# One batch's tile sums computed as matrix products, and the next batch's pooling softmax and memories moved into the kernel's head

## The chip, the core and the metric

The kernel runs on one core of a Trainium2 chip. The core has a matrix engine (PE; the profile shows its weight loads apart as PEld), a vector engine (DVE), a scalar engine (ACT), GpSimd (POOL) and a sync engine (SP) that here issues every transfer. Each engine runs its own list of instructions in order and waits on semaphores for the others. The metric is the device time of one execution in microseconds.

## The reference

Eight batches of memory attention feed a Fourier mixing layer and a feed-forward layer. Cut to what matters:

```
a      = softmax(phi, over the 32 memories)            # phi: 8 x 8 x 576 x 32
k_m    = einsum('bhsm,bhsd->bhmd', a, k)               # 32 memories per head
v_m    = einsum('bhsm,bhsd->bhmd', a, v)
attn   = softmax(q @ k_m^T / 8)                        # 576 x 32 per head
x      = attn @ v_m, the eight heads side by side      # 8 x 576 x 512
u      = x + real(fft(fft(x, axis=seq), axis=model))
un     = (u - mean(u)) / sqrt(var(u) + 1e-6)
out    = u + relu(un @ w_ch1) @ w_ch2                  # 512 -> 2048 -> 512
```

The code subtracts the maximum of phi over the 576 positions (the softmax over axis 2 normalises over positions), and the sums are normalised with 1e-9 added.

## The kernel before

**Layout.** Heads are taken in pairs, so a batch has four pairs (`NG`), 128 partitions each. A batch first makes the pooling weights: phi is transposed on PE (tiles `pf`, `pl`), DVE takes maxima, ACT exponentiates into `pht`, and PE transposes back (`pt_e`) into `et`. Then each pair's memories are products of k and v with `et` (`pm`), its scores are products of q with the memories (`psc`), and `pair_scores` softmaxes them. The Fourier transform over positions is a product with a cosine and a sine table (`ct`); with cosines even and sines odd, the six tiles of a pair's attention weights `a` are first added and subtracted into even and odd parts `eo` (L524 to L531), split into f16 high and low parts `aeo` (L534 to L538), and multiplied in `spectrum` (`pa`, evicted into `at` at L618 and L619). `values` prepares the pooled values (`vh`), and `mix_m` and `mix_x` (`pp_t`, `px_t`) make the rows `u` in `uring`.

**Precision.** Batches 0 and 1 (`NX = 2`) work in float32; later ones split float32 into two f16 parts and make three f16 products.

**Feed-forward.** The rows are taken in 18 chunks of 256 (`CH = 2` tiles). Chunk 0 is computed in float32 directly (`ffn1_direct` L744, `ffn2_direct` L761) while the weights are being turned from 64-bit words into floats: `to_f32` (L842 to L855) for the eight units of W1 and of W2, one ACT and three DVE instructions per unit or half unit. Afterwards `split_w1` and `prepare_w2` split them into f16 high and low parts, and chunks 1 to 17 run three f16 products for each (L274 `ph` and L797 `po`).

**Order.** A framework's scheduler sets the order on each engine from the order in which the code issues, from priorities and from explicit edges (`issue_after`). The generator `background()` issues a batch's work in steps; the loop over chunk 0's eight units issues two steps of the second batch after each unit, and the chunks after it go on so. `GATE1` and `GATE2` name marks behind which a unit's conversion is issued: W2's unit 0 behind `at0`, the last spectrum eviction of the first batch.

**Fillers.** `keep_busy(n)` (L246) issues products of a zero tile of 512 columns into a PSUM tile that nobody reads. `KEEP` gives the counts: 8 before the first data, 18, 4 and 3 in the first batch's pooling, 14 in `values` of batch 0, and 19 ahead of chunk 0's normalised input `pt_unT` (L726).

**Second batch before the change.** `pooling_weights(1)` is issued behind `at0`, so its transposes, exponentials and copies run at the start of chunk 0, and its four pairs' memories run inside chunk 0, with masking by DVE (L396, L398). Its phi and its k, v, q come by transfers behind those of weight units 1 and 2 (L283, L295).

Of the kernel before, what the change touches and what calls it, by code (L numbers as in the profile page):

```python
# [10 lines left out]
F32 = mybir.dt.float32  # L11
F16 = mybir.dt.float16
# [121 lines left out]
def kernel(  # L134
# [43 lines left out]
    uring = const.tile([P, NU, DM], F32, name="uring")  # L178
    zeros = uring[:, NU - 1].bitcast(F16)[:, :DM]
    nc.vector.memset(zeros, 0.0)  # L180
    identf = const.tile([P, P], F32, name="identf")
    make_identity(nc, identf)
    make_identity(nc, ident)
    warm = const.tile([P, 1], F32, name="warm")
    nc.vector.memset(warm, 0.0)
# [192 lines left out]
    def memory_f32(b, g, r, vmf, parts):  # L378
# [15 lines left out]
        if 0 in parts:  # L394
            kmf = share[:, g * 64 : g * 64 + 64] if b == 0 else tiny("kmf", 64, 2)
            nc.vector.tensor_tensor(out=kmf, in0=pm[:, 0:64], in1=mk[:, 0:64], op=ALU.mult)  # L396
        if 1 in parts:
# [6 lines left out]
        return kmf  # L404

    def pair_memory(b, g, r, vmf, ivs):

# [67 lines left out]
    def pair_scores(b, g, q, sc, km, es, aeo):  # L475
# [37 lines left out]
        nc.vector.reciprocal(out=sm, in_=sm)  # L513
        eng = nc.gpsimd if b else nc.vector
        eng.tensor_tensor(out=a, in0=a, in1=sm.unsqueeze(2).to_broadcast([P, 12, M]), op=ALU.mult)  # L515

        av = a.rearrange("p (t h) m -> p t (h m)", h=2)
        ahl = ahring[:, (b * NG + g) % NAH]
        if b == 0 and g > 0:
            ahl = ud.rearrange("p l t c -> p (l t c)")[:, (g - 1) * 5 * P : g * 5 * P]  # L520
            ahl = ahl.rearrange("p (t c) -> p t c", t=5)
        nc.scalar.copy(out=ahl[:, :, 0:64], in_=av[:, 0:5])
        nc.gpsimd.tensor_tensor(out=ahl[:, :, 64:128], in0=av[:, 0:5], in1=ahl[:, :, 0:64], op=ALU.subtract)
        for i, op in ((12, ALU.add), (16, ALU.subtract)):  # L524
            eng.tensor_tensor(out=a2[:, i : i + 4], in0=a[:, 0:4], in1=a[:, 4:8], op=op)  # L525
        ap = a2[:, 8:].rearrange("p (t s h) m -> p t s (h m)", s=2, h=2)
# [3 lines left out]
        )  # L530
        nc.vector.tensor_tensor(out=eo[:, :, 1], in0=ap[:, :, 0], in1=ap[:, :, 1], op=ALU.subtract)  # L531
        hi, lo = (aeo[:, l].rearrange("p t e h c -> p (t e h) c")[:, :, g * M : g * M + M] for l in range(2))
        eov = eo.rearrange("p t e (h m) -> p (t e h) m", m=M)
        marks[f"a{b}_{g}"] = nc.scalar.copy(out=hi, in_=eov)  # L534
        nc.gpsimd.tensor_tensor(out=lo[:, 4:], in0=eov[:, 4:], in1=hi[:, 4:], op=ALU.subtract)
# [201 lines left out]
    def ffn1_direct(j):  # L737
# [3 lines left out]
        for f in range(UB):  # L741
            ph = ps1.tile([P, CH, P], F32, tag="h", name=f"ph_0_{j}_{f}", padded_shape=[P, 4, P])
            for k in range(NK):
                nc.tensor.matmul(  # L744
                    ph, lhsT=w[:, k, f * P : (f + 1) * P], rhs=unTs[0][:, k], start=(k == 0), stop=(k == NK - 1)
                )
            nc.scalar.activation(h[:, f], ph, AF.Relu)

# [181 lines left out]
    def background():  # L930
# [3 lines left out]
        for b in range(B):  # L934
# [6 lines left out]
            if b == 0:  # L941
# [63 lines left out]
    def load_unit(n, parts, w, stages):  # L1005
        marks["load"] = marks.get("load", marks["q"])
        parts[n] = load_stage(w[n], stage_area(stages[n]))

    def load_weights(n):

        for parts, w, stages in ((parts_w1, w1, W1_STAGE), (parts_w2, w2, W2_STAGE)):
            if n not in parts:
                load_unit(n, parts, w, stages)


    for what in [1, 'w1', 2, 3, 'w2']:
        if what == "w1":
            load_unit(0, parts_w1, w1, W1_STAGE)
            marks["q"] = marks["load"]
        elif what == "w2":  # L1020
            load_unit(0, parts_w2, w2, W2_STAGE)
            marks["q"] = marks["load"]
        else:
            first.append(load_pair(0, what))
            marks["load"] = marks["q"]
    marks["load"] = marks["q"]
    with tc.issue_after(marks["load"].ins):
        vts = [load_vt()]
        marks["load"] = nc.sync.dma_start(out=ct, in_=ct_d)
    for j in range(3):  # L1030
        load_weights(j)

# [137 lines left out]
```

## Time and profile before

| | us |
|---|---|
| median of 3 runs | 951.38 (951.35 to 952.24) |
| the profiled execution | 951.47 |
| its span, first to last instruction | 949.6 |
| transposes of chunk 0's input start | 50.50 |
| chunk 0's first product `ph` starts | 53.41 |
| chunk 0's last product `po` ends | 126.2 |
| the last `po` ends | 945.8 |

The span is what the trace covers; 1.9 us of the execution lie around it. In the profile's groups a row names line, engine, operation, tiles, shapes and count, then busy time, mean duration in ns, and idle time ahead of the group with its releaser. Rows of the timeline begin with start and duration in us; their count merges neighbours, and a float32 product counts twice, as it shows two records. In rows of windows the stretch stands first, then its length, then busy times with counts, the granted clock of PE as a share, the busy share of the DMA engines, and GB/s. DVE's durations overlap by about 0.1 us: the next instruction starts that much before the one ahead ends.

### The profile page before, as it was taken

How to read it: one execution, taken by the hardware profiler on the slowest of the kernel's cores; microseconds unless marked ns; L12 is line 12 of the kernel's file. 1: busy time of each engine (PE TensorE's matmuls, PEld its weight loads, DVE VectorE, ACT ScalarE, POOL GpSimd, SP SyncE). 2: the span in 40 equal slices, each digit the busy share in tenths (PEclk: the TensorE clock that was granted, in tenths of full speed). 3: DMA queues.
4: the chain of work that ended last, by engine and by line, in shares of the span. 5: the costliest groups of instructions: out<-in, count | busy, mean ns of one | idle time of the engine just before them, and what ended most of it. 6: DMA issues, size and time to landing. Idle time of an engine off the chain costs nothing.

```text
span 949.6 us, 18892 instructions
## 1 busy us (share of the span) xinstructions
PE 932.5 (98%) x7764; PEld 660.0 (70%) x7764; DVE 558.5 (59%) x1307; ACT 457.5 (48%) x912; POOL 216.3 (23%) x245
## 2 busy tenths in 40 slices
PE   9899999999999999999999999999999999999998
PEld 6566777577777777776767677777776667666664
DVE  5999878677565665667524676667656765221111
ACT  3565667865365545654514554755446544311110
POOL 1200442534122232323100241223221331200000
PEclk9999999999999999999999999999999999999999
DMA  9848551454126231643102631273223311110000
GB/s 343 308 170 266 178 145 19 86 134 103 43 45 172 55 93 26 156 113 93 23 23 54 143 96 48 48 155 95 45 68 72 82 20 36 39 45 23 1 23 23
DMA packets 115958, 88.08 MB, mean 93 GB/s; under 512 B 100384, under 2 KB 100384, under 8 KB 113824
## 3 DMA queue, kind: packets, MB, share of 16 engines
q1 hardware_dynamic: 115872, 86.87, 34.4%
q8 instruction: 61, 1.00, 0.4%
q14 instruction: 25, 0.20, 0.1%
HBM read 58.15 MB, written 9.44 MB: 71 GB/s over the span
## 4 chain that ended last, share of the span: by engine, by line
PE 88%; DVE 6%; DMA 2%; ACT 1%; POOL 1%; issue 1%; SPq 0%; DVEq 0%; POOLq 0%; ACTq 0%
PE po L797 36%; PE ph L274 35%; PE ph L744 3%; PE pm L274 3%; PE po L761 3%; PE pp_t L274 2%; PE psc L274 2%; PE px_t L274 2%; DMA w1t<-in_w 1%; PE pa L607 1%; PE pp_t L650 1%; PE pf L348 1%; PE pv L580 1%; POOL w2s L916 0%; DMA unring<-ud 0%
## 5 line engine op out<-in xcount | busy, mean ns | idle before, releaser
L274 PE MATMUL ph<-unring,w1t 128*128 128x256 f16 x3264 | 388.9, 273 | 2.9 <-DVE scratch L241 1.3
L797 PE MATMUL po<-w2s,hring 128*128 128x512 f16 x1632 | 378.5, 379 | 1.6 <-POOL w2s L916 1.6
L274 PEld LDWEIGHTS <-w1t 128*128 128x128 f16 x3264 | 314.9, 98 | 66.4 <-issue 4.8
L797 PEld LDWEIGHTS <-hring 128*128 128x128 f16 x1632 | 156.9, 98 | 160.0 <-issue 2.4
L788 DVE SCALAR_TENSOR_TENSOR hring<-ph,hring 128x512 f16<-128x512 f32 x136 | 93.1, 685 | 148.3 <-ACT hring L787 148.1
L787 ACT ACTIVATE hring<-ph 128x512 f16<-128x512 f32 x136 | 80.3, 591 | 166.4 <-PE ph L274 163.5
L710 POOL TENSOR_TENSOR scratch<-scratch,small 128x1 f32<-128x1 f32 x36 | 24.1, 670 | 197.6 <-DVE scratch L709 118.4
L515 POOL TENSOR_TENSOR aring<-aring,scratch 128x384 f32<-128x384 f32 x28 | 23.3, 833 | 183.5 <-DVE scratch L513 172.2
L274 PEld LDWEIGHTS <-stg 128*128 128x128 f16 x1152 | 44.7, 98 | 8.1
L509 ACT ACTIVATE aring<-aring,scratch 128x384 f32<-128x384 f32 x24 | 14.7, 612 | 63.1 <-DVE aring L508 63.1
L731 POOL TENSOR_TENSOR ud<-un,ud 128x1024 f16<-128x1024 f32 x17 | 36.7, 2158 | 30.6 <-ACT ud L730 30.6
L432 POOL TENSOR_TENSOR stg<-rawt,stg 128x640 f16<-128x640 f32 x12 | 18.3, 1524 | 86.9 <-ACT rawt L431 86.9
L274 PE MATMUL pm<-et,stg 128*128 128x64 f16 (+1 forms) x780 | 36.8, 199 | 0.0
L499 DVE TENSOR_REDUCE scratch<-psc 128x12 f32<-128x384 f32 x32 | 17.7, 554 | 32.4 <-PE pm L274 18.0
L534 ACT CAST aeo<-eo 128x384 f16<-128x384 f32 x30 | 15.3, 511 | 42.2 <-DVE eo L531 42.2
L686 DVE SCALAR_TENSOR_TENSOR uring<-px_t,scratch,share 128x256 f32<-128x256 f32 (+1 forms) x80 | 34.3, 478 | 0.1
L809 DVE SCALAR_TENSOR_TENSOR uring<-po,small,uring 128x512 f32<-128x512 f32 x34 | 24.2, 743 | 16.7 <-PE po L797 16.7
L672 DVE SCALAR_TENSOR_TENSOR share<-pp_t,scratch,small 128x257 f32<-128x257 f32 (+1 forms) x48 | 21.1, 483 | 20.9 <-ACT small L669 20.9
L525 POOL TENSOR_TENSOR aring<-aring 128x128 f32<-128x128 f32 x56 | 32.6, 602 | 2.1
L744 PE MATMUL ph<-unring,w1t 128*128 128x256 f32 x128 | 31.4, 389 | 0.0
L527 DVE TENSOR_TENSOR eo<-aring 128x128 f32<-128x128 f32 x29 | 28.1, 968 | 5.2 <-POOL aring L525 5.2
L536 DVE SCALAR_TENSOR_TENSOR aeo<-aeo,small,eo 128x128 f16<-128x128 f16 x30 | 24.3, 809 | 11.3 <-ACT aeo L534 11.2
(242 smaller groups left out, 1219.3 us busy)
## 6 DMA issues: line engine op xcount, KB each, us to landing
rawt<-in_raw SPq DMA_DIRECT2D x15, 640.0 KB, 5.2
stg<-in_raw SPq DMA_DIRECT2D x15, 640.0 KB, 4.8
out<-uring SPq DMA_DIRECT2D x36, 256.0 KB, 2.1
stg<-in_w SPq DMA_DIRECT2D x7, 1024.0 KB, 5.0
rawt<-in_raw SPq DMA_DIRECT2D x15, 384.0 KB, 3.5
stg<-in_raw SPq DMA_DIRECT2D x15, 384.0 KB, 3.1
phs<-in_raw SPq DMA_DIRECT2D x32, 160.0 KB, 4.1
w2s<-in_w SPq DMA_DIRECT2D x4, 1024.0 KB, 9.8
```

Of the source, the lines that this page charges most:

```text
L274: m = nc.tensor.matmul(out, lhsT=lhsT, rhs=rhs, start=start, stop=stop)
L525: eng.tensor_tensor(out=a2[:, i : i + 4], in0=a[:, 0:4], in1=a[:, 4:8], op=op)
L527: nc.vector.tensor_tensor(out=eo[:, 1:3, 0], in0=ap[:, 1:3, 0], in1=ap[:, 1:3, 1], op=ALU.add)
L536: marks[f"s{b}_{g}"] = nc.vector.scalar_tensor_tensor(out=lo[:, :4], in0=hi[:, :4], scalar=mk[:, 64:65], in1=eov[:, :4], op0=ALU.mult, op1 ...
L686: nc.vector.scalar_tensor_tensor(out=u[rows, hs], in0=px[rows, hs], scalar=igx[rows], in1=tm[rows, w * NJ + half : w * NJ + half + 256], o ...
L731: marks[f"ul{c}"] = nc.gpsimd.tensor_tensor(out=ud[:, 1], in0=un, in1=ud[:, 0], op=ALU.subtract)
L744: nc.tensor.matmul(ph, lhsT=w[:, k, f * P : (f + 1) * P], rhs=unTs[0][:, k], start=(k == 0), stop=(k == NK - 1))
L761: nc.tensor.matmul(po[t], lhsT=h[:, f, t], rhs=w[:, f], start=(j == 0 and f == 0), stop=(j == NW - 1 and f == UB - 1),)
L787: nc.scalar.activation(h[:, 0], phv, AF.Relu)
L788: nc.vector.scalar_tensor_tensor(out=h[:, 1], in0=phv, scalar=0.0, in1=h[:, 0], op0=ALU.max, op1=ALU.subtract)
L797: nc.tensor.matmul(po[t], lhsT=hs[j][:, lh, f * 2 + t], rhs=w2s[:, j * UB + f, lw, :], start=(j == 0 and f == 0 and i == 0), stop=(j == NW ...
L809: nc.vector.scalar_tensor_tensor(out=u, in0=po[t], scalar=cout if c else 0.5, in1=u, op0=ALU.mult, op1=ALU.add)
```

## The change

Three things change, and with them how the head is filled.

1. **Tile sums as products, batch 0.** DVE's and POOL's additions on `a` are not made for batch 0. Instead `a` is split into f16 high and low parts for all six tiles, and `tile_sums` adds up the even and odd parts in PSUM: products with the identity and with `minus`, its negative, one each for the high and the low part. The splits that follow read PSUM. POOL's remainders there go to DVE, and batch 0's masking of memories goes from DVE to ACT (two instructions of 64 partitions each, into tiles cleared before).
2. **Second batch in the head.** Its phi and its k and v are loaded right after the first batch's data (into areas that are free until chunk 0), its softmax over phi (`next_weights`) is issued after the tile sums, and its memories (`next_memories`) after chunk 0's normalisation; POOL masks them when a pair needs them. The scaling of the exponentials and the copies of the transposed ones go from DVE to ACT. Only q is loaded for it later.
3. **W2's first unit** is gated behind `s0_1`, the last part of pair 1's sums, in place of `at0`.

Fillers now multiply halves of the float identity, 256 columns each and twice as many; the 14 and the 19 go. Relu of chunk 0 gets a high priority.

```
-KEEP = [8, 18, 14, 0, 19, 4, 3]
+KEEP = [8, 18, 0, 0, 0, 4, 3]
-GATE2 = [["at0"]] + [["un1", "uh0"]] * 7
+GATE2 = [["s0_1"]] + [["un1", "uh0"]] * 7
...
-        pt = ps2.tile([P, 512], F32, tag="o", name=f"keep_{len(kept)}")
-        kept.append(pt)
-            for _ in range(n):
-                nc.tensor.matmul(pt, lhsT=zeros[:, :P], rhs=zeros, start=True, stop=True)
+            for _ in range(2 * n):
+                nc.tensor.matmul(idle, lhsT=unread[:, :P], rhs=unread, start=True, stop=True)
...
+        nt = 5 if b else 6
...
-        nc.scalar.copy(out=ahl[:, :, 0:64], in_=av[:, 0:5])
-        nc.gpsimd.tensor_tensor(out=ahl[:, :, 64:128], in0=av[:, 0:5], in1=ahl[:, :, 0:64], op=ALU.subtract)
+        nc.scalar.copy(out=ahl[:, :, 0:64], in_=av[:, 0:nt])
+        (nc.gpsimd if b else nc.vector).tensor_tensor(
+            out=ahl[:, :, 64:128], in0=av[:, 0:nt], in1=ahl[:, :, 0:64], op=ALU.subtract
+        )
+        if b == 0:
+            return ahl
...
+    def tile_sums(g, ahl, aeo):
+        pe = ps1.tile([P, 512], F32, tag="h", name=f"pe_{g}")
+        eo = pe[:, : 3 * P].rearrange("p (n c) -> p n c", c=2 * M)
+        for group in (
+            (
+                (ident, 0, slice(2, 6), 0, P),
+                (ident, 1, slice(2, 6, 2), 0, P),
+                (ident, 2, slice(2, 4), 0, P),
+                (ident, 3, slice(2, 6, 3), 0, P),
+                (minus, 1, slice(3, 6, 2), 0, P),
+                (minus, 2, slice(4, 6), 0, P),
+                (minus, 3, slice(3, 5), 0, P),
+            ),
+            (
+                (ident, 4, slice(0, 2), 0, 96),
+                (ident, 4, slice(1, 2), 96, P),
+                (ident, 5, slice(0, 1), 0, P),
+                (minus, 5, slice(1, 2), 0, P),
+            ),
+        ):
+            for i, (w, t, o, a, z) in enumerate(group):
+                for l in range(2):
+                    src = ahl[a:z, t, l * 64 : l * 64 + 64]
+                    marks["pe"] = nc.tensor.matmul(
+                        eo[:, o], lhsT=w[a:z],
+                        rhs=src.unsqueeze(1).to_broadcast([z - a, eo[:, o].shape[1], 64]),
+                        start=(i + l == 0), stop=(i + l == len(group)), skip_group_check=True,
+                    )
+        even_odd(0, g, eo.rearrange("p n (h m) -> p (n h) m", m=M), aeo, nc.vector)
...
+    def next_weights():
...
+            nc.scalar.activation(pht_next[:, g, : 4 * P], pf[g], AF.Exp, bias=m, accum_out=su[:, g : g + 1])
...
+            nc.scalar.activation(pht_next[:, g], pht_next[:, g], AF.Copy, scale=su[:, 2 + g : 3 + g])
...
+            nc.scalar.copy(out=et_next[g][:, :4], in_=pt.rearrange("p (t c) -> p t c", c=P))
...
+    def next_memories():
+        for g in range(NG):
+            kv = kv_next[g].rearrange("p (t w c) -> p t w c", t=NST, w=2)
+            pm = ps1.tile([P, 512], F32, tag="h", name=f"pm_1_{g}")
...
+            nc.scalar.copy(out=pm_next[:, g], in_=pm[:, :P])
...
-            return q, None, memory_f32(b, g, r, vmf, range(2)), 1.0 / 8.0
+            return q, None, kept_memory(g, vmf), 1.0 / 8.0
...
-            nc.scalar.activation(h[:, f], ph, AF.Relu)
+            with tc.high_priority(3000):
+                nc.scalar.activation(h[:, f], ph, AF.Relu)
...
                 for g in range(NG):
                     memory_f32(b, g, first[g], vmf, [1])
+                for g in range(NG):
+                    tile_sums(g, ahl[g], aeo)
+                next_weights()
...
-    for what in [1, 'w1', 2, 3, 'w2']:
+    for what in (1, 'w1', 2, 3, 'w2', 'v', 'c', 'p', 'm'):
...
-    keep_busy(KEEP[4])
     unTs = {0: norm_chunk(0)}
-    after(["at0"], pooling_weights, 1)
+    next_memories()
+    load_weights(2)
```

`kept_memory` makes the masked memories of a pair from the copies `pm_next` with two POOL instructions.

More of the change, by code (lines that the diff above doesn't have):

```diff
@@ L178 @@
     uring = const.tile([P, NU, DM], F32, name="uring")
-    zeros = uring[:, NU - 1].bitcast(F16)[:, :DM]
-    nc.vector.memset(zeros, 0.0)
     identf = const.tile([P, P], F32, name="identf")
+    unread = identf.bitcast(F16)
     make_identity(nc, identf)
     make_identity(nc, ident)
+    minus = const.tile([P, P], F16, name="minus")
+    nc.gpsimd.tensor_scalar(out=minus, in0=ident, scalar1=-1.0, scalar2=None, op0=ALU.mult)
     warm = const.tile([P, 1], F32, name="warm")
@@ L198 @@
     et32 = et.rearrange("p g l t c -> p (g l t c)").bitcast(F32).rearrange("p (g t c) -> p g t c", g=2, t=NST)
+    un32 = unring.rearrange("p a l t k c -> p (a l t k c)").bitcast(F32)
+    pht_next = un32[:, : 2 * S].rearrange("p (g s) -> p g s", g=2)
+    et_next = [w1t[:, j].rearrange("p l k c -> p (l k c)").bitcast(F32)[:, : NST * P] for j in (0, NW)]
+    et_next = [t.rearrange("p (t c) -> p t c", t=NST) for t in et_next]
+    ur = uring.rearrange("p a c -> p (a c)")
+    phi_next = stg[:, 1].bitcast(F32)[:, : NST * NG * 2 * M].rearrange("p (t g c) -> p t g c", t=NST, g=NG)
+    kv_next = [
+        stg[:, 2].bitcast(F32)[:, :KV],
+        hring[:, 4:8].rearrange("p a l f c -> p (a l f c)").bitcast(F32)[:, :KV],
+        ur[:, 2 * DM : 2 * DM + KV],
+        ur[:, 2 * DM + KV : 2 * DM + 2 * KV],
+    ]
+    pm_next = uring[:, NU - 1].rearrange("p (g c) -> p g c", g=NG)
+    for t in et_next:
+        nc.gpsimd.memset(t[:, NST - 1], 0.0)
     nc.gpsimd.memset(half, -0.5)
@@ L204 @@
     share = const.tile([P, 2 * NJ], F32, name="share")
+    nc.gpsimd.memset(share[:, : 64 * NG], 0.0)
+    nc.gpsimd.memset(vmf, 0.0)
     rings, taken = {}, [0]
@@ L228 @@
     kept = []
+    idle = ps2.tile([P, 512], F32, tag="o", name="idle")[:, : 2 * P]
     def norm_scale(dst_s, dst_i, sq, n, expo, key):
@@ L395, in memory_f32 @@
             kmf = share[:, g * 64 : g * 64 + 64] if b == 0 else tiny("kmf", 64, 2)
-            nc.vector.tensor_tensor(out=kmf, in0=pm[:, 0:64], in1=mk[:, 0:64], op=ALU.mult)
-        if 1 in parts:
+            if b == 0:
+                for i in (0, 1):
+                    d = slice(i * 64, i * 64 + 64)
+                    nc.scalar.activation(kmf[d, i * M : i * M + M], pm[d, i * M : i * M + M], AF.Copy, scale=2.0**-EB)
+            else:
+                nc.vector.tensor_tensor(out=kmf, in0=pm[:, 0:64], in1=mk[:, 0:64], op=ALU.mult)
+        if 1 in parts and b == 0:
+            for i in (0, 1):
+                d = slice(i * 64, i * 64 + 64)
+                nc.scalar.activation(
+                    vmf[d, g, :, i * M : i * M + M],
+                    pm[d, 64 + i * M : 64 + i * M + M].unsqueeze(1).to_broadcast([64, 2, M]),
+                    AF.Copy,
+                    scale=2.0**-EB,
+                )
+        elif 1 in parts:
             nc.vector.tensor_tensor(
@@ L1013, in load_weights, with load_next @@
                 load_unit(n, parts, w, stages)
-    for what in [1, 'w1', 2, 3, 'w2']:
+    def load_next(dst, src):
+        with tc.issue_after(marks["load"].ins):
+            marks["load"] = nc.sync.dma_start(out=dst, in_=src)
+    marks["load"] = marks["q"]
+    for what in (1, 'w1', 2, 3, 'w2', 'v', 'c', 'p', 'm'):
         if what == "w1":
             load_unit(0, parts_w1, w1, W1_STAGE)
-            marks["q"] = marks["load"]
         elif what == "w2":
             load_unit(0, parts_w2, w2, W2_STAGE)
+        elif what == "v":
+            with tc.issue_after(marks["load"].ins):
+                vts = [load_vt()]
+            marks["load"] = marks["vt"]
+        elif what == "c":
+            load_next(ct, ct_d)
+        elif what == "p":
+            for g in range(NG):
+                load_next(phi_next[:, :, g], raw[1, g, :, KV:KVP].rearrange("p (t c) -> p t c", t=NST))
+        elif what == "m":
+            for g in range(NG):
+                load_next(kv_next[g], raw[1, g, :, :KV])
+        else:
             marks["q"] = marks["load"]
-        else:
             first.append(load_pair(0, what))
             marks["load"] = marks["q"]
[L1026 to L1031, printed above, removed]
+    load_weights(1)
     bg = background()
```

85 lines of the change are left out of this document (70 added, 15 removed).

## The prediction

> **What bounds the kernel now.** I read the page's head first, then the table of waits of PE (waiter, released by: us in total, times, longest), then the windows (stretch; busy us of PE, PEld, DVE, ACT, POOL; granted clock; DMA share; GB/s).
>
> ```profile
> span 949.6 us, 18892 instructions
> PE 932.5 (98%) x7764; PEld 660.0 (70%) x7764; DVE 558.5 (59%) x1307; ACT 457.5 (48%) x912; POOL 216.3 (23%) x245
> ```
>
> ```profile
> PE as_vq L224 <- ACT share L552: 3.1, 1, 3.1
> PE pt_unT L726 <- DVE un L711: 2.3, 1, 2.3
> PE po L797 <- POOL w2s L916: 1.6, 1, 1.6
> PE ph L274 <- DVE scratch L241: 1.3, 1, 1.3
> ...
> PE ph L274 <- DVE at L619: 1.2, 1, 1.2
> ```
>
> ```profile
> 13.30:53.40 40.10, 33.54 (x289) 0.94 0.77 291
> 53.40:107.60 54.20, 54.20 (x248) 37.74 (x247) 54.20 (x101) 33.69 (x58) 3.05 (x3) 0.98 0.62 218
> 130.00:190.00 60.00, 55.26 (x507) 41.76 (x505) 45.06 (x127) 46.54 (x86) 24.89 (x24) 1.00 0.32 70
> 190.00:945.00 755.00, 755.00 (x6524) 529.70 (x6523) 403.06 (x927) 336.63 (x691) 164.35 (x185) 1.00 0.29 68
> ```
>
> From 190 us to 945 us PE never waits: 755.00 of 755. So the end is set by how much PE has to do and by how much of the first 190 us is not its work. That loss is what the change can win back. It has four parts: waits in the head from 13.3 to 53.4 (40.10 - 33.54 = 6.6 us), waits from 130 to 190 (60.00 - 55.26 = 4.7 us), fillers that compute nothing, and work at a halved clock. The second thing to see is the row 53.40:107.60: there **DVE is as full as PE**, 54.20 of 54.20. It turns W1 and W2 into floats for the first chunk, so PE may not run much faster there than DVE.
>
> **The change, part by part.** Fillers: KEEP[2] goes from 14 to 0, and the call with KEEP[4] = 19 is gone. The windows of the filler tile alone (PE busy, clock):
>
> ```profile
> 31.80:36.50 4.70, 4.61 (x14) 0.69 1.06 335
> 43.90:48.30 4.40, 4.26 (x19) 1.00 0.11 44
> ```
>
> That takes out 4.61 + 4.26 = **-8.9 us**. The other 33 fillers become 66 of half the width, the same columns.
>
> Tile sums as products: per pair 22 products in f16, four pairs. Two move 256 columns, fourteen 128, six 64. Rows of PE for such widths (start, us, engine line, tile, count):
>
> ```profile
> 148.92 2.78 PE L274 MATMUL ph<-unring,w1t 128*128 128x256 f16 x24 [1.19 <-DVE at L619]
> 43.02 1.06 PE L274 MATMUL px_t<-vbdt,attnT 128*128 128x128 f16 x16
> 186.93 1.04 PE L274 MATMUL pm<-et,stg 128*128 128x64 f16 x30
> ```
>
> The last product of a group overlaps the next group, so I take 0.11, 0.06 and 0.03 us each: 0.22 + 0.84 + 0.18 = 1.24 us a pair, **+4.9 us**. A single product could cost as little as 0.03 or as much as 0.07 us (1.06 / 16), so 3 to 6 us. In exchange DVE loses the adds of L525 to L531 in the head and gains the f16 remainders from POOL; that is the chain to the last aeo, counted next.
>
> The head's waits. This is PE of the changed kernel just ahead of the first chunk (pt_e: the second batch's exponentials transposed back; pm: its memories, 40 float products; pt_unT: the chunk's input):
>
> ```order
> L469 MATMUL pt_e_0_515<-identf,unring 128x128 x4
> L471 MATMUL pl_488<-identf,unring 64x128
> L469 MATMUL pt_e_1_524<-identf,unring 128x128 x4
> L481 MATMUL pm_0_711<-w1t,stg 128x64 x4
> L471 MATMUL pl_488<-identf,unring 64x128
> L481 MATMUL pm_0_711<-w1t,stg 128x64 x6
> L481 MATMUL pm_1_723<-w1t,hring 128x64 x10
> L481 MATMUL pm_2_735<-w1t,uring 128x64 x10
> L861 MATMUL pt_unT_694<-identf,un 128x128 x4
> L481 MATMUL pm_3_747<-w1t,uring 128x64
> L861 MATMUL pt_unT_705<-identf,un 128x128 x4
> ```
>
> Before, the 19 fillers and a wait of 2.3 us stood ahead of pt_unT; now pt_e and pm_0 to pm_2 do, all of them work that ran inside the first chunk. On ACT the second batch's softmax stands between the steps of the first (L753: spectrum out of PSUM, L456 and L457: exponentials, L466: their scaling, L804: what the first mix needs):
>
> ```order
> L753 ACTIVATE at<-pa_1_0_613 128x2x145
> L456 ACTIVATE unring,scratch<-pf_1_495,scratch 128x512
> L457 ACTIVATE unring,scratch<-pl_488,scratch 128x64
> L753 ACTIVATE at<-pa_1_1_623 128x2x145
> L284 COPY vbdt<-pt_vbd_0_634 128x1024
> L284 COPY attnT<-pt_attnT_3_0_644 128x640
> L757 COPY at<-at 128x8x31
> L466 ACTIVATE unring<-unring,scratch 128x576 x2
> L804 ACTIVATE small<-pp_t_651,scratch 128x255
> ```
>
> Before, none of L456, L457 and L466 stood there: the four L618, the two copies, L622 and L669 followed one another. What they cost (DVE and ACT rows; then on PE a pair's memories, pt_e, a mix, and the first chunk's start):
>
> ```profile
> 40.45 1.77 DVE L619 SCALAR_TENSOR_TENSOR at<-pa,at 128x290 f16<-128x290 f32 x4
> 56.38 0.66 ACT L314 ACTIVATE phs<-pf,scratch 128x512 f32<-128x512 f32 x1
> 180.72 0.79 ACT L370 ACTIVATE elt<-phs,scratch 128x576 f16<-128x576 f32 x1
> 119.02 2.23 PE pm L274 x20
> L329 PE MATMUL pt_e<-identf,phs 128*128 128x128 f32 x8 | 1.2, 272 | 0.0
> 41.71 1.48 PE L274 MATMUL pp_t<-vh,at 128*128 128x257 f16 x12
> 53.41 2.77 PE L744 MATMUL ph<-unring,w1t 128*128 128x256 f32 x8
> ```
>
> The spectrum ended at 42.2 us (40.45 + 1.77). With two exponentials and their short partners (about 2 us) ahead I put it at 45; the two scalings (up to 0.79 each) put L804 some 4 us later than before. The transposes pt_e then start at 47.5, pm_0 at 49, and three memories at 2.2 us each carry pt_unT to 55.6 and, behind pm_3 and half a mix, the first chunk's ph to 59.5 us, against 53.41. PE's work between 13.3 and 59.5 is then 33.5 - 8.9 (fillers) - 0.8 (clock, below) + 4.9 + 8.9 (four memories) + 1.1 (pt_e) + 0.7 (half a mix) = 39.4 of 46.2 us: 6.8 us of waits, about as many as the 6.6 before, **+0.2 us**, to be read as 0 +- 2. The memories and pt_e are no term by themselves: they leave the first chunk again, one for one.
>
> The halved clock (third number from the end):
>
> ```profile
> 31.30:34.70 3.40, 3.40 (x15) 1.59 (x13) 3.40 (x13) 2.46 (x6) 1.83 (x3) 0.50 1.00 398
> 48.30:51.70 3.40, 1.20 (x10) 1.09 (x11) 2.00 (x7) 0.47 (x1) 1.17 (x2) 1.00 0.00 0
> 51.70:55.20 3.50, 3.50 (x15) 3.15 (x14) 2.65 (x6) 3.50 (x5) 0.00 (x0) 0.51 0.02 7
> ```
>
> The first slow interval held fillers mostly. The last, behind 3.4 us with 1.20 us of work, held real work: about 0.8 us lost before 53.41 and 0.9 after it. With memories in the place of that wait it should not come: **-1.7 us**. [...]
>
> Waits after 55 us. Those of 130 to 190 come from the second batch's pairs being late (pair sums, spectrum) and from W2's split on POOL. Their products run some 20 us earlier now, so I let most of the 4.7 go. In their place DVE comes. Between the last L711 and the last W2 float at 107.5 it was busy all but 1.7 of 57.7 us:
>
> ```profile
> 49.80:107.50 57.70, 56.04 (x104) 0.97 0.59 205
> L845 DVE SCALAR_TENSOR_TENSOR w1t<-stg,w1t 128x1024 int32<-128x1024 int32 x4 | 4.9, 1222 | 0.0
> L308 DVE TENSOR_REDUCE scratch<-pf 128x1 f32<-128x512 f32 x2 | 1.4, 686 | 1.4 <-PE pf L348 1.4
> L325 DVE TENSOR_SCALAR phs<-phs,scratch 128x576 f32<-128x576 f32 x2 | 1.0, 518 | 0.0
> L334 DVE COPY et<-pt_e 128x512 f32<-128x512 f32 x2 | 1.4, 693 | 0.0
> L499 DVE TENSOR_REDUCE scratch<-psc 128x12 f32<-128x384 f32 x3 | 1.7, 558 | 3.2 <-PE psc L274 3.2
> L508 DVE TENSOR_TENSOR aring<-psc,scratch 128x384 f32<-128x384 f32 x3 | 1.7, 553 | 0.1
> L511 DVE TENSOR_REDUCE scratch<-aring 128x12 f32<-128x384 f32 x3 | 1.7, 553 | 1.7 <-ACT aring L509 1.7
> L881 DVE SCALAR_TENSOR_TENSOR w1t<-w1t,small 128x1024 f16<-128x1024 f32 x2 | 2.6, 1292 | 0.0
> ```
>
> Now that stretch also holds the second batch's softmax, since its products are early; here DVE, around W1's last unit (w1t from hring and uring):
>
> ```order
> L600 TENSOR_TENSOR aring<-psc_2_1105,scratch 128x384
> L264 RECIPROCAL small<-small 128x1
> L639 SCALAR_TENSOR_TENSOR aeo<-aeo,small,eo 128x4x32
> L981 SCALAR_TENSOR_TENSOR w1t<-hring,w1t 128x512
> L981 SCALAR_TENSOR_TENSOR w1t<-uring,w1t 128x512
> L626 TENSOR_TENSOR eo<-aring 128x2x64
> L261 TENSOR_SCALAR small<-scratch 128x1 x2
> L980 TENSOR_SCALAR w2s<-w2s 128x1024
> L627 SCALAR_TENSOR_TENSOR eo<-aring,small 128x64
> L630 TENSOR_TENSOR eo<-aring 128x3x64
> L594 TENSOR_REDUCE scratch<-psc_3_1177 128x12
> L991 SCALAR_TENSOR_TENSOR w1t<-hring,w1t 128x512
> ```
>
> Before, the last unit's floats stood ahead of every row of that softmax. Durations less the 0.1 us by which DVE's instructions overlap give: 54.9 us before (56.0 less the two L711 at its start), less the pooling (L308, L325, L334 and ten scalars: 4.6) and 0.4 of memory masks, plus eleven reductions and subtractions at 0.47 (5.2), the small sums (2.7), a third split (1.2) and some 24 more scalars at 0.13 (3.1): 62.1 us. ACT converts unit 1 only behind the copies of pt_unT, so DVE starts at 58.4 and has W2's last unit at 120.5, W1's 4 us earlier at 116.5. PE's pace in the chunk:
>
> ```profile
> 59.57 1.89 PE L744 MATMUL ph<-unring,w1t 128*128 128x256 f32 x8
> 61.30 1.88 PE L761 MATMUL po<-w2s,hring 128*128 128x512 f32 x4
> 108.82 1.28 PE psc L274 x12
> ```
>
> A half unit is 1.73 us (61.30 - 59.57). Without waits PE wants W1's last unit at 114.5: 59.5, plus 14 halves of ph (24), 13 of po (22), mixes (3), four pair scores (5) and small ones (1). W2's it wants 7.7 us later. That is nearly level: 2 us of waits if DVE keeps its pace, 4 to 5 with gaps as between L508 and L511 (1.7 us of waiting for ACT over three). With 1 to 2 us elsewhere I take 6 us against 4.7, **+1.3 us**; the bounds are 0 (DVE always ahead) and 13 (the waits of L499 and L511, 4.9 us over three pairs, so 6.5 over four, and POOL's rows as long again).
>
> SP's queue is moved past by eight loads of 3.2 MB for the second batch, ahead of W1's and W2's unit 1:
>
> ```profile
> 20.00:30.00 10.00, 7.94 (x72) 7.82 (x71) 9.93 (x31) 5.49 (x11) 2.29 (x3) 1.00 1.02 416
> 16.81 0.33 SPq L830 DMA_DIRECT2D w2s<-in_w  x1
> ```
>
> At 416 GB/s they take 7.7 us; unit 1, issued to 16.81 before, lands near 37 and is wanted near 57. That cover is 20 us. Unit 2's stages come free with pf and pm_0, near 51, for a use past 60. The new gate s0_1 of W2's unit 0 costs nothing: its floats stand before the mix now and after it before.
>
> Sum: -8.9 + 4.9 + 0.2 - 1.7 + 1.3 = -4.2 us. The profiled execution took 951.47 us, of which the span is 949.6; the median shown is 951.38, 0.1 less. 951.4 - 4.2 = **947.2 us**.
>
> **Rivals.** (1) DVE is ahead all along and the later waits vanish: the last term becomes -4.7 to -0.7, hence 941.2 to 945.2. For it: W1's units 1 to 3 are ready 3 to 8 us early by the same counting. Against: the level race at unit 7. (2) **DVE ends the first chunk**: POOL's remainders and the pair softmax stretch it, and ph of unit 7 waits. From 5.5 us of wait more than the 4.7 of before (10.2 us in all, W1's last unit past 123 us) the kernel is slower. The row of L511 with its idle time speaks for it; the bound of 13 gives 954.2. (3) The clock halves again in the head, since real work runs in broken pieces between 41 and 48 us: each interval of 3.4 us costs 1.7 us, at worst on two, so 949 to 950.6. For it: 1.20 us of work in 3.4 us brought it last time. Against: I count 5 us of work in those 7. [...] (4) The change doesn't fill the waits: the memories queue ahead of pt_unT and the head grows by more than they leave behind. With 3 us more of waits: 950.2.
>
> **How the numbers follow.** Forecast (945.2 to 949.6): 0.43. Rival 1: 0.22. Rivals 3 and 4 with part of 2 (949.6 to 953.3): 0.21. Rival 2 beyond: 0.14. The range 941.5 to 952.5 leaves out some 0.04 below and 0.16 above. Within 0.2% (1.9 us, about what a measurement of this kernel can tell from no change) means 949.5 to 953.3. Faster 0.65, same 0.21, slower 0.14.
>
> **What would show it.** In the changed profile: PE without fillers after 13.3 us; its table of waits with as_vq and pt_unT gone and waits on the memories' copies or on at instead; first ph L879 near 59.5 us; the clock at 1.00 from 48 to 56; DVE full from 58 to 121 and PE waiting for w1t or w2s floats near 115; nothing from 190 on. A first ph past 63 us, or a wait for w1t floats past 8 us, would prove me wrong on the slow side; PE at 10.0 of 10 from 60 to 180 on the fast side.

## The result and the profile after

| | before | after |
|---|---|---|
| median of 20 runs, us | 952.10 | 962.66 |
| lowest to highest, us | 951.22 to 953.51 | 951.25 to 965.33 |

The ratio of the means is 1.0085, 95% interval 1.0062 to 1.0108: **slower by 0.85%**, where 947.2 us was forecast with a range up to 952.5. The median hides the shape. Six of the 20 runs took 951.25 to 953.06 us at a mean granted clock of 0.995 or 0.996, fourteen took 960.03 to 965.33 us at 0.982 to 0.988, and none lay between. I call them short and long executions. The profiled execution of the changed kernel was a short one (952.3 us), so its page shows only half of the matter: a changed kernel that gained nothing. What made the others long is in the experiments.

The short execution, first its head and then its windows (columns as before: stretch; busy us of PE, PEld, DVE, ACT, POOL; clock; DMA share; GB/s):

```profile
span 950.5 us, 19067 instructions
PE 932.7 (98%) x7852; PEld 665.9 (70%) x7852; DVE 557.9 (59%) x1271; ACT 462.8 (49%) x936; POOL 217.8 (23%) x250
```

```profile
13.30:57.80 44.50, 40.36 (x441) 37.15 (x440) 31.58 (x87) 29.62 (x73) 3.18 (x7) 1.00 0.94 338
57.80:130.00 72.20, 65.48 (x283) 44.83 (x282) 69.31 (x134) 49.79 (x85) 24.11 (x19) 0.93 0.55 181
130.00:190.00 60.00, 58.48 (x498) 43.17 (x498) 44.04 (x105) 41.76 (x76) 23.79 (x22) 1.00 0.27 66
190.00:945.00 755.00, 755.00 (x6548) 530.02 (x6545) 406.27 (x930) 337.48 (x692) 161.27 (x185) 1.00 0.30 69
```

The first chunk's ph starts at 57.80 us. Up to there PE waits 44.50 - 40.36 = 4.1 us, less than before. But PE now waits 72.20 - 65.48 = 6.7 us in the first chunk, where it never waited, and the clock is 0.93 there. From 190 us on PE is full, as before. Its table of waits begins like this:

```profile
PE ph L879 <- DVE w1t L991: 6.7, 2, 3.4
...
PE psc L292 <- issue: 1.2, 1, 1.2
```

The rows of the chunk on PE (start, us, line, tile, count, wait and releaser) show two events of one kind, below a row at the full clock:

```profile
83.56 2.75 PE L879 MATMUL ph<-unring,w1t 128*128 128x256 f32 x12
...
98.81 6.60 PE L879 MATMUL ph<-unring,w1t 128*128 128x256 f32 x16 [3.27 <-DVE w1t L991]
105.25 3.17 PE L897 MATMUL po<-w2s,hring 128*128 128x512 f32 x7
...
123.93 1.13 PE L879 MATMUL ph<-unring,w1t 128*128 128x256 f32 x4 [3.45 <-DVE w1t L991]
124.90 3.36 PE L897 MATMUL po<-w2s,hring 128*128 128x512 f32 x4
128.05 3.01 PE L879 MATMUL ph<-unring,w1t 128*128 128x256 f32 x12
```

PE waits 3.27 us for W1's floats of unit 5 and 3.45 for those of unit 7, and **behind each wait the clock is halved** (0.50 of full speed from 98.25 to 104.20 us and from 125.95 to 128.50, by windows of 0.85 us): 16 records of ph take 6.60 us, and the four of po 3.36. At the full clock they take 3.7 (2.75 / 12 x 16) and 1.88 (row 61.30 in the prediction). With unit 5 that is 2.9 us lost, with unit 7 1.5 + 0.3, the last from 3.01 against 2.75.

Why DVE is late for unit 5 can be read from its own rows and POOL's:

```profile
91.35 2.15 DVE L980 TENSOR_SCALAR w2s<-w2s 128x512 int32<-128x512 int32 x1
...
95.02 2.60 DVE L981 SCALAR_TENSOR_TENSOR w2s<-hring,w2s 128x512 int32<-128x512 int32 x1
97.54 1.21 DVE L991 SCALAR_TENSOR_TENSOR w1t<-stg,w1t 128x1024 uint32<-128x1024 uint32 x1
```

```profile
90.10 3.11 POOL L866 TENSOR_TENSOR ud<-un,ud 128x1024 f16<-128x1024 f32 x1
94.83 2.25 POOL L1015 TENSOR_TENSOR w1t<-w1t 128x1024 f16<-128x1024 f32 x1 [1.62 <-ACT w1t L1014]
```

Two conversions of half a unit, which should cost less than one of a whole (0.67 and 1.2 us), end just behind an instruction of POOL (POOL's ends 93.2 and 97.1 us, DVE's 93.5 and 97.6). Only the second of these, L1015, is a split of W1; L866 is the remainder of the next chunk's input. Before, POOL did both 16 to 17 us later (107.37 and 110.91 us), when DVE was done with its conversions (the last began at 106.23 and took 1.24 us).

The wait for unit 7 looks in part like an echo of the first. A row of ACT and one of DVE between the two:

```profile
105.45 0.38 ACT L883 ACTIVATE hring<-ph 128x256 f32<-128x256 f32 x1 [1.40 <-PE ph L879]
```

```profile
107.93 0.69 DVE L980 TENSOR_SCALAR w2s<-w2s 128x1024 int32<-128x1024 int32 x1 [2.50 <-ACT w2s L978]
```

DVE stands idle for 2.50 us until ACT has converted the next words (L978, 106.77 to 107.90 us), and that instruction stands in ACT's queue behind a relu (L883) that waits for PE's slowed products. How much of the 3.45 us this makes was not tested.

### The profile page after: what moved, and what is told of

Read it like the earlier page. It is cut to its first block, busy times and chain, and to the rows that moved or that the text cites. A ratio compares the mean times of both kernels' runs of the same rounds, so it can differ in the third digit from the quotient of the medians.

```text
span 950.5 us, 19067 instructions
## 1 busy us (share of the span) xinstructions
PE 932.7 (98%) x7852; PEld 665.9 (70%) x7852; DVE 557.9 (59%) x1271; ACT 462.8 (49%) x936; POOL 217.8 (23%) x250
## 4 chain that ended last, share of the span: by engine, by line
PE 88%; DVE 6%; ACT 2%; issue 2%; DMA 1%; POOL 1%; DVEq 0%; ACTq 0%; POOLq 0%
PE ph L292 37%; PE po L933 36%; PE pm L292 3%; PE pp_t L292 2%; PE psc L292 2%; PE px_t L292 2%; PE pa L742 1%; PE ph L879 1%; DVE w2s L981 1%; PE idle L270 1%; DVE w1t L991 1%; PE pm L481 1%; PE po L897 1%; PE pf L366 1%; PE pp_t L785 1%
## 5 line engine op out<-in xcount | busy, mean ns | idle before, releaser
L866 POOL TENSOR_TENSOR ud<-un,ud 128x1024 f16<-128x1024 f32 x17 | 37.1, 2185 | 29.5 <-ACT ud L865 29.5
L879 PE MATMUL ph<-unring,w1t 128*128 128x256 f32 x128 | 33.4, 412 | 6.7 <-DVE w1t L991 6.7
L879 PEld LDWEIGHTS ph<-unring,w1t 128*128 128x128 f32 x128 | 26.1, 209 | 14.9 <-DVE w1t L991 7.8
L594 DVE TENSOR_REDUCE scratch<-psc 128x12 f32<-128x384 f32 x32 | 17.5, 547 | 29.9 <-PE pm L292 15.4
L637 ACT CAST aeo<-eo 128x384 f16<-128x384 f32 x28 | 14.3, 511 | 40.9 <-DVE eo L630 40.8
L865 ACT CAST ud<-un 128x1024 f16<-128x1024 f32 x17 | 17.8, 1044 | 33.1 <-DVE un L846 30.7
L292 PE MATMUL pm<-et,stg 128*128 128x64 f16 (+1 forms) x740 | 32.5, 195 | 1.1 <-DMA et<-elt 1.1
L897 PE MATMUL po<-w2s,hring 128*128 128x512 f32 x64 | 31.6, 626 | 0.0
```

Of the source, the lines that this page charges most:

```text
L292: m = nc.tensor.matmul(out, lhsT=lhsT, rhs=rhs, start=start, stop=stop)
L866: marks[f"ul{c}"] = nc.gpsimd.tensor_tensor(out=ud[:, 1], in0=un, in1=ud[:, 0], op=ALU.subtract)
L879: nc.tensor.matmul(ph, lhsT=w[:, k, f * P : (f + 1) * P], rhs=unTs[0][:, k], start=(k == 0), stop=(k == NK - 1))
L897: nc.tensor.matmul(po[t], lhsT=h[:, f, t], rhs=w[:, f], start=(j == 0 and f == 0), stop=(j == NW - 1 and f == UB - 1),)
```

## The experiments

Where a time of the kernel before or a ratio to it stands beside a run, it was taken on the same chip in the same minutes. In all it ran 90 times for these comparisons: 89 runs between 950.77 and 953.52 us, one at 959.16.

**1. A long execution.** The changed kernel, unaltered, twice more. The expectations count seven short runs and thirteen long ones; the times on record give six and fourteen.

> The changed kernel unaltered, once more with a profile. Of its 20 runs 7 took 951.25 to 953.06 us at a mean granted clock of 0.995, and 13 took 960.03 to 965.33 us at 0.982 to 0.988; the profile at hand is of the first group. Theory A (clock): a long execution shows the same waits as the short one, and some seven more intervals of about 3.4 us at half clock with PE full (7 x 1.7 = 12 us). Theory B (waits): a long execution shows 10 to 13 us more in the table of waits of PE, from DVE or a DMA that came late, and the lower clock is a companion of these.

> The same kernel a second time, so that at least one of the two profiles is likely to fall in the long group (13 of 20 did). As for the first: theory A expects about 963 us from some seven more intervals at half clock with the waits unchanged, theory B 10 to 13 us more of waits; an execution near 952 us tells nothing.

Measured: 965.22 us at 0.982 and 952.57 at 0.995 (before 952.28). The first is a long execution. Its PE, then its ACT, then windows of 1.7 us:

```profile
13.99 1.28 PE L292 MATMUL pm<-et,stg 128*128 128x64 f32 x10
17.53 2.06 PE L292 MATMUL psc<-share,rawt 128*128 128x64 f32 x12 [2.26 <-issue]
```

```profile
15.93 1.22 ACT L978 ACTIVATE w1t<-w1t 128x512 f32<-128x512 f32 x2 [3.21 <-DMA w1t<-in_w]
17.05 0.79 ACT L417 ACTIVATE share<-pm 64x32 f32<-64x32 f32 x4
```

```profile
15.30:17.00 1.70, 0.00 (x0) 0.00 (x0) 0.38 (x1) 1.07 (x2) 0.00 (x0) 1.00 1.01 405
17.00:18.70 1.70, 1.17 (x9) 1.20 (x10) 1.67 (x5) 0.80 (x5) 0.00 (x0) 0.89 1.02 416
18.70:20.40 1.70, 1.70 (x10) 1.70 (x10) 1.39 (x4) 0.00 (x0) 0.00 (x0) 0.50 1.03 434
...
44.20:45.90 1.70, 1.70 (x22) 1.48 (x21) 0.63 (x3) 0.69 (x2) 0.00 (x0) 0.58 0.99 352
45.90:47.60 1.70, 1.70 (x30) 1.52 (x28) 1.70 (x6) 1.68 (x3) 0.00 (x0) 1.00 0.98 376
```

Read it from ACT: L417, the change's new place for the mask of the first pair's K memory, stands in ACT's queue **behind** L978, the conversion of W1's first unit, and that waits for its DMA. PE's first pair scores (psc) wait for the mask, 2.26 us here. Their row names no releaser ("issue"); that it is the mask is read from the order of these rows, and run 3 shows it. In the short execution W1 was there 1 us earlier; its rows of ACT and PE:

```profile
14.97 1.22 ACT L978 ACTIVATE w1t<-w1t 128x512 f32<-128x512 f32 x2 [2.18 <-DMA w1t<-in_w]
```

```profile
16.56 1.52 PE L292 MATMUL psc<-share,rawt 128*128 128x64 f32 x12 [1.24 <-issue]
```

After the wait the clock goes to half at 18.33 us (0.89 of a window of 1.7 leaves 0.37 us at half) and stays there until 45.63: 27.3 us, eight intervals of 3.41, though **PE is busy without a gap in all of them**. Up to 40.0 us its work is products of 64 columns, all but one record; the clock comes back at the end of the first interval without them (42.2 to 45.6 us, the tile sums above all, up to 256 columns wide). First ph starts at 71.17 us instead of 57.80; these 13.4 us are about the 12.9 by which the spans differ.

The half clock of runs 5, 9 and 10 below lasts 23.9, 10.2 and 30.7 us, seven, three and nine times 3.41, so in these four profiles it lasts whole steps of this length. Theory A holds, with eight intervals for the seven expected: PE's waits between 13.3 and 945 us grow only from 12.4 to 14.3 us, where theory B asked for 10 to 13 more.

Before, the mask was DVE's, and its row stood ahead of the conversion there:

```profile
14.54 0.23 DVE L396 TENSOR_TENSOR share<-pm,small 128x64 f32<-128x64 f32 x1 [1.12 <-PE pm L274]
15.94 0.43 DVE L844 TENSOR_SCALAR w1t<-w1t 128x512 int32<-128x512 int32 x1 [1.18 <-ACT w1t L842]
```

**2. The fillers put back.**

```diff
-KEEP = [8, 18, 0, 0, 0, 4, 3]
+KEEP = [8, 18, 14, 0, 19, 4, 3]
+    keep_busy(KEEP[4])
     unTs = {0: norm_chunk(0)}
```

> The two sets of fillers are put back: 14 between the pair transposes of the first batch and 19 ahead of the norm of the first chunk (each as two of 256 columns), all else as in the change. If the long executions come from a clock that halves in the head because nothing fills it any more, this kernel has one group of times only, at 955 to 960 us (951.3 plus at most 8.9 us of fillers, less what falls into waits), at a clock of 0.995 or more. If they come from the first chunk, where PE waits for DVE, the two groups stay, each later by 2 to 9 us.

Measured: one of six runs at 952.03, five at 962.18 to 965.85; ratio 1.0099 (1.006 to 1.0139). The fillers come behind the tile sums, at 44 us, too late for a clock that fell at 17.5 (0.65 in the window from 17.00 to 18.70). So the missing fillers are not why it falls there. In this profile a wait of 0.89 us was enough.

**3. Only the order on ACT.** The mask of the first pair goes ahead of W1's conversions.

```diff
-GATE1 = [["et0"]] + [["un1", "uh0"]] * 7
+GATE1 = [["km0"]] + [["un1", "uh0"]] * 7
-                    nc.scalar.activation(kmf[...
+                    marks[f"km{g}"] = nc.scalar.activation(kmf[...
```

> Only the order on ACT is changed: the first pair's K mask (L417) now stands ahead of the conversions of W1's first unit (L978), which wait for its DMA; in the change it stands behind them. Theory A: the wait of PE ahead of the first pair scores (1.1 us in a short execution, 2.3 us in a long one, where the clock then stays at half for 27 us) is what makes the two groups. Then psc starts at 15.4 to 15.6 us, the clock is 1.00 until 90 us in every run, and there is one group at 950 to 953 us (952.3 less 1.1). Theory B: the halving has another cause (the phase of the clock's window, the fillers on the identity); then some runs stay at 960 us or more at a clock below 0.99.

Measured: nine of eleven runs at 950.37 to 951.55, two at 961.34 and 961.94 (before 951.38). The wait ahead of psc is gone, and most long executions with it. The two left need another wait. It was caught in the profile of run 5, which has the same order on ACT:

```profile
15.16 1.50 PE L292 MATMUL psc<-share,rawt 128*128 128x64 f32 x12
18.02 1.40 PE L292 MATMUL pm<-et,w1t 128*128 128x64 f32 x10 [1.36 <-DMA w1t<-in_raw]
```

Here the third pair's data are late, PE idles 1.36 us, and the clock is at half from 19.1 to 43.0 us (0.61 in the window from 18.70 to 20.40, 0.86 from 42.50 to 44.20).

**4. Fillers over the wait.** The order stays; PE gets work instead.

```diff
+            for _ in range(16 if b == 0 and g == 0 else 0):
+                marks["pe"] = nc.tensor.matmul(psc[:, : 2 * P], lhsT=unread[:, :P], rhs=unread, start=True, stop=True)
             for t in range(6):
                 mm(psc[:, t * 64 : t * 64 + 64], lhsT=q[:, t * P : (t + 1) * P], ...)
```

> The change, with 16 fillers of 256 columns (1.75 us at the full clock) put right ahead of the first pair scores, into their own tile, so that PE works while it would wait; the order on ACT stays. Theory A: no run above 957 us; 952.3 plus at most 0.65 (1.75 less the 1.1 of waiting) = 953. Theory B: long executions stay at 962 to 966 us.

Measured: 949.03 us, all seven runs at 948.74 to 949.44; ratio to before 0.9973 (0.9963 to 0.9984). Theory A holds: no long execution. That it is 4 us under the expected 953 goes with DVE's order in the first chunk, which came out otherwise: between 57.8 and 130 us PE waits 5.1 us in place of 6.7, at a clock of 0.98 in place of 0.93. POOL still splits W1 here, yet the wait at unit 5 is gone: only one wait of ph is left in the table, 3.6 us ahead of the row at 120.12 us. So the order alone can remove one of the two waits.

**5. W1 split by DVE alone** (with the order of run 3).

```diff
-L2 = [2, 4, 6]
+L2 = []
```

> The ACT order of e3, and W1's units 2, 4 and 6 are split by DVE and no longer by POOL. It asks about the two waits of 3.3 and 3.5 us for W1's floats in the first chunk. Theory lock: they come from DVE instructions that are stretched while POOL works (2.15 and 2.60 us where 0.35 and 0.68 are usual, around 91 to 97 us); then the stretches beside POOL's splits (1.9 + 1.8 us) go, two splits of 1.3 come to DVE ahead of unit 7, and the waits come to 5 to 6 us or less. Theory load: DVE simply has too many instructions; then 2.6 to 3.9 us more of them make the waits 9 to 10 us and the time 953 to 956 us.

Measured: five of ten runs at 943.3 to 945.14, five long ones at 954.72 to 956.87. Against run 3 the short ones gain some 7 us and the long ones some 6, although DVE has more to do: the theory of load falls. In its profile, a long one, the waits for W1's floats are 1.3 us. The expectation puts both stretched instructions beside splits on POOL; by the rows above only the second is, so the edit by itself takes away one of the two meetings.

**6. The second batch later**, with the order of run 3.

```diff
-STEPS = 2
+STEPS = 1
```

> The ACT order of e3, and the background of the second batch advances by one step per unit instead of two, so that its pair softmax comes to DVE behind W1's last unit. If the pair softmax in the first chunk is what makes PE wait for W1's floats (6.7 us) and lets the clock halve behind each wait (3.0 + 1.7 us), both go, and some 1 to 5 us of waits come back between 130 and 190 us: 951.2 - 11.4 + 1 to 5 = 941 to 945 us. If the conversions alone fill DVE, the waits stay at 5 us or more and the time at 949 to 952 us.

Measured: 962.11 us (955.44 to 967.38). This kernel no longer computes the reference's output, so the time is a hint only. The wait for W1's floats in the first chunk fell to 2.9 us, but PE then waited 5.6 us for the second chunk's transposed input between 170 and 190 us. Not a way out.

**7 and 8. Both corrections together**: run 4's fillers with POOL's splits taken away; then half as many fillers, and the order of run 3 with them.

```diff
-L2 = [2, 4, 6]
+L2 = []
+            for _ in range(16 if b == 0 and g == 0 else 0):
...
+            for _ in range(8 if b == 0 and g == 0 else 0):
```

> The 16 fillers ahead of the first pair scores (as in the run with fillers there, 949.0 us, one group) and W1's units split by DVE alone (as in the run without POOL's splits, whose short executions took 943.3 us and whose long ones 955 to 957). If the two causes are separate, they add up: one group of times at 943 to 945 us (943.3 plus at most 1.75 of fillers), the clock at 0.998 or more, waits for W1's floats under 2 us, and no DVE instruction between 85 and 100 us stretched to over 2 us beside a split on POOL. If the stretched instructions are not what delays W1's floats, the first chunk keeps waits of 5 us and the time stays at 948 to 950 us.

> The same with half of the fillers (8, 0.9 us) and the first K mask ahead of W1's conversions on ACT, so that PE no longer waits ahead of the first scores and can idle only for the DMA of the third pair (1.4 us in the long execution seen, of which the fillers take 0.9). Theory: an idle of 0.5 us does not let the clock fall; one group at 942.5 to 944.5 us. If the clock falls on any idle beside narrow products, long executions at 953 to 957 us remain.

Measured: **944.78 us** (944.69 to 945.12, five runs), ratio 0.9925 (0.9911 to 0.9938); and **944.50 us** (943.67 to 945.14), ratio 0.9921 (0.9908 to 0.9934). Before: 952.06. No long execution, the clock at 0.998 or more. Of the first one, windows, then the first row of PE's waits, then DVE's two halved conversions with the floats of unit 5 (L993) and one more row, and a row of POOL:

```profile
90.00:100.00 10.00, 10.00 (x41) 7.24 (x39) 10.00 (x19) 5.20 (x8) 3.59 (x2) 1.00 0.75 229
100.00:120.00 20.00, 16.59 (x68) 10.01 (x67) 20.00 (x39) 15.56 (x29) 8.86 (x9) 1.00 0.52 161
120.00:130.00 10.00, 10.00 (x50) 6.83 (x49) 10.00 (x27) 6.48 (x12) 3.85 (x6) 1.00 0.32 108
```

```profile
PE po L899 <- ACT hring L885: 3.1, 2, 2.4
```

```profile
90.64 0.40 DVE L982 TENSOR_SCALAR w2s<-w2s 128x512 int32<-128x512 int32 x1
...
91.03 1.20 DVE L993 SCALAR_TENSOR_TENSOR w1t<-stg,w1t 128x1024 uint32<-128x1024 uint32 x1
...
92.69 2.62 DVE L1019 SCALAR_TENSOR_TENSOR w1t<-w1t,small 128x1024 f16<-128x1024 f32 x1
...
96.37 0.68 DVE L983 SCALAR_TENSOR_TENSOR w2s<-hring,w2s 128x512 int32<-128x512 int32 x1
```

```profile
91.00 3.23 POOL L868 TENSOR_TENSOR ud<-un,ud 128x1024 f16<-128x1024 f32 x1 [0.65 <-ACT ud L867]
```

PE is full from 90 to 100, waits 3.4 us between 100 and 120, and the clock stays at 1.00. The two conversions that took 2.15 and 2.60 us take 0.40 and 0.68. The first of them escapes by its place alone: it is done at 91.04, as POOL's L868 begins. That instruction is the remainder of the next chunk's input, no split, and it stays; DVE's split beside it is still stretched (2.62 us, where the same row at 100.42 takes 1.27), but it now lies behind the floats that PE wants. For the second conversion the split beside it is gone. What was not separated: taking POOL's splits away also let the order on DVE come out anew, so how much of the 4 to 7 us is the stretching and how much the order stays open.

**9. What brings the clock back.**

```diff
+            for _ in range(24 if b == 0 and g == 2 else 0):
+                marks["pe"] = nc.tensor.matmul(psc[:, : 2 * P], lhsT=unread[:, :P], rhs=unread, start=True, stop=True)
```

> The change, with 24 fillers of 256 columns (2.6 us at the full clock, 5.2 at half) ahead of the third pair's scores, behind the wait. Theory C: once at half, the clock stays there because products of 64 columns, which spend half of their time on loading weights, do not count as enough work; wide products would bring it back at the next window. Then long executions come to 955 to 959 us (952.3 plus 2.6 of fillers, plus two to three intervals of half clock at 1.7 us less what the head's later waits take), not 963, and short ones to 953 to 955. Theory D: the clock stays low for a fixed time, or until DMA traffic ends; then long executions are at 964 to 968 us.

Measured: 953.63 to 957.71 us, median 955.30, six runs. PE and windows:

```profile
16.48 2.23 PE L292 MATMUL psc<-share,rawt 128*128 128x64 f32 x12 [0.59 <-issue]
...
25.33 3.77 PE L577 MATMUL psc<-identf 128*128 128x256 f16 x24
28.94 1.45 PE L292 MATMUL psc<-share,w1t 128*128 128x64 f32 x12
```

```profile
17.00:18.70 1.70, 1.70 (x10) 1.70 (x10) 1.26 (x3) 0.00 (x0) 0.00 (x0) 0.53 1.04 418
...
27.20:28.90 1.70, 1.70 (x17) 1.49 (x15) 1.67 (x6) 1.03 (x3) 0.00 (x0) 0.96 0.87 188
```

The clock falls at 17.1 us behind an idle of only 0.59, and comes back at 27.3, some 2 us after the first wide product, three intervals in place of eight. DMA traffic goes on (0.88 of the DMA engines' time from 25.50 to 27.20 us, 0.87 from 27.20 to 28.90), so theory D falls and C's forecast holds. The reason that C gives is not shown by it. That the products of 64 columns spend half of their time on loading weights was the author's estimate; the trace has PEld as full as PE beside them (1.70 us each in the window from 17.00). And the fillers differ from the scores in type (f16 for f32) as well as in width. The short execution of the changed kernel parts these two. Behind its first wait in the first chunk the clock is at half from 97.8 to 104.7 us (by windows of 0.85 us), two intervals, and only the second is filled with work without a gap, f32 products of 256 columns; at 105.25 po is at the full clock again (0.45 us a record). So one full interval of wide f32 products did what six of narrow ones in run 1 didn't, and the width, not the type, is what these runs point to.

**10. The fillers taken out of the kernel before**, and nothing else.

```diff
-KEEP = [8, 18, 14, 0, 19, 4, 3]
+KEEP = [8, 18, 0, 0, 0, 4, 3]
```

> The kernel before, with nothing but its two sets of fillers taken out (14 and 19 of 512 columns, 4.61 and 4.26 us of PE time). The prediction counted them as 8.9 us to be won, against work that comes in their places. If the time they take is all waiting anyway, nothing is won: waits of PE on ACT and DVE grow by 8 to 9 us, one or two intervals of half clock are added, and the time is 951 to 955 us. If some of it was on the path, the time falls to 945 to 950 us.

Measured: eight of ten runs at 953.39 to 955.31, two at 961.36 and 962.44; before 952.06; ratio 1.0042 (1.0023 to 1.0062). Taking out the 8.9 us of fillers alone wins nothing: the short runs have their median at 954.7 us, 2.6 us above the kernel before, at a clock of 0.989 to 0.991 where that has 0.996 to 0.998. The profile is of a long run; a row of PE and a window:

```profile
17.90 1.96 PE L274 MATMUL pm<-et,w1t 128*128 128x64 f32 x10 [0.77 <-DMA w1t<-in_raw]
```

```profile
47.60:49.30 1.70, 1.70 (x16) 1.52 (x15) 1.64 (x3) 1.23 (x4) 0.00 (x0) 0.57 0.00 0
```

The kernel before can fall into the same hole (0.77 us of idle, then half clock from 18.4 us (0.90 in the window from 17.00 to 18.70) up to 49.1, with further idle of PE from 37 us on). With its fillers 1 of 90 runs was long, without them 2 of 10; so few don't settle how far the fillers keep it out.

**11. POOL's splits in the kernel before.**

```diff
-L2 = [2, 4, 6]
+L2 = []
```

> The kernel before, with W1's units 2, 4 and 6 split by DVE instead of POOL, and nothing else. It asks what of the 7 us won by the two corrected versions of the change (944.5 and 944.8 us) would have been there without the change. The kernel before has no wait for W1's floats in its first chunk, so if the gain belongs to the change, this kernel is at 950 to 953 us; if POOL's splits cost as much in the kernel before, it is at 945 to 948 us.

Measured: ten of twelve runs at 951.10 to 952.68, two at 959.01 and 959.36, before 951.55; ratio 1.0012 (0.999 to 1.0034). Nothing is won there, so what POOL's splits cost in runs 7 and 8 they cost only with the change. Run 7's other correction, fillers ahead of the first pair's scores, was not tried in the kernel before, which has no wait at that place (psc follows pm without a gap at 15.45 us). So the 7 us belong to the change, once its two faults are mended, as far as these runs tell. Why two of these runs were long stays open.

## Why the prediction was wrong

Term by term, in the short execution that was profiled (952.3 against 951.47 us, +0.8):

| term of the sum | predicted | measured |
|---|---|---|
| fillers | -8.9 | -8.9 (none after 13.3 us; but see run 10) |
| tile sums | +4.9 | at most +6.2 |
| waits in the head | +0.2 | 4.1 - 6.6 = -2.5 |
| halved clock in the head | -1.7 | -1.7 |
| waits after it | +1.3 | 6.7 + 1.5 - 4.7 = +3.5 |
| halved clock behind these | none | 2.9 + 1.5 + 0.3 = +4.7 |

They add up to +1.3. The tile sums are the busy time of their 88 products (window of the tile pe alone; PE, DVE, ACT), whose ends overlap other work:

```profile
27.00:36.00 9.00, 6.17 (x88) 2.02 (x6) 1.91 (x4) 1.00 1.03 377
```

- **Right**: PE stays full from 190 us on; as_vq's and pt_unT's waits go; POOL's split of W2 is no longer waited for; DVE is nearly full in the first chunk (69.31 of 72.20 us) and PE waits there for W1's floats, at unit 5 as well as at the unit 7 that was named. The head was even better than counted, ph at 57.80 for 59.5.
- **Mis-sized**: "Waits after 55 us". The mechanism was named, rival 2, but its durations came from a stretch in which POOL was nearly idle (49.80 to 107.50 us, POOL busy for 3.54 of 57.70). The change brought POOL's work forward onto the same stretch (24.11 of 72.20), and DVE's instructions got up to 1.9 us longer beside it: 2.15 us in place of the 0.40 of run 7, 2.60 in place of 0.68. That they end just behind POOL's instructions is what the rows show; by what POOL's work would hold DVE up was not shown. And a wait of 3.3 us was priced as a wait, not as a wait and one or two intervals at half clock behind it. These two terms, +3.5 and +4.7 where +1.3 was counted, are why even the short executions gained nothing.
- **The step that failed**: "With memories in the place of that wait it should not come: **-1.7 us**". The half clock was looked for only at 48 to 56 us (and by rival 3 at 41 to 48, "at worst on two" intervals). In the long execution of run 1 it came at 18, for eight intervals; 14 of 20 runs were long, and that is the whole difference between a change that is level (the short runs) and one that is 0.85% slower. Behind this lies an edit that got no price: the move of the first batch's mask from DVE to ACT stands in no term of the sum (the 0.4 us of memory masks there are the second batch's, in the first chunk). What stands ahead of it in ACT's queue, a conversion that waits for 1 MB of W1, was not asked.
- Rival 3 had the right cause at the wrong place. Its measure came from the trace of before, 1.20 us of work in 3.4. Shorter gaps sufficed here: beside the 2.26 us of run 1 also idles of 0.59 (run 9), 0.77 (run 10), 0.89 (run 2) and 1.36 us (run 5). And windows in which PE was busy without a gap (1.70 of 1.70 us in run 1) did not lift it.

## What to carry to other kernels

When a small operation moves to another engine, read which instruction stands ahead of it in that queue and what that one waits for; a DMA there made the wait vary from run to run here (1.12, 1.24 and 2.26 us in three executions of one kernel). A wait on PE can cost more than its length, here most of all where the products around it were narrow (2.26 us ahead of 64 columns led to eight intervals at half clock, 27.3 us, and 3.27 us ahead of 256 columns to two): price the clock behind it, and put a few wide products there rather than trust that PE is "busy". Fillers that seem to cost 8.9 us may cost nothing (run 10), and a kernel whose runs fall into two groups needs a profile of each.

## What the hardware showed unexpectedly

Products of 128x64 f32 without a gap held the full clock (1.00 in the short execution from 16.6 to 27.6 us), but lost it with under 1 us of idle (0.59, 0.77 and 0.89 us seen) and didn't win it back in six intervals that they filled (run 1, 18.3 to 38.8 us). With wide ones it came back: after some 2 us of 256 columns in f16 (run 9), and in the first chunk after one interval that f32 products of 256 columns filled (98.8 to 104.7 us). The rows suggest why: 10 records of 64 columns take 1.28 us and keep PEld as full as PE (11.00 us each in the 11.00 from 16.6), while 8 of 256 columns take 1.89. Four times the columns take less than twice the time per record; if a column costs the same in both, columns take at most about half of the time in the narrow ones (an estimate from these two rows). That the clock follows this share was only inferred. And idles of 1.12 and 1.24 us in the two short executions profiled left the clock at 1.00; what parts them from the shorter ones that sufficed was not shown.
